# The last block of a fused attention and mixture kernel: where GpSimd multiplies, the order of two exponentials, and a product in two column halves

## The chip, the cores and the metric

The kernel runs on one core of one Trainium2 chip. The time is device microseconds (us) of one execution; of the kernel before three runs are known, 574.03, 574.24 and 574.85 us, median 574.24 us.

## What is computed

Three layers follow each other. Chunked attention takes chunks of 32 queries, each with a window of 56 keys and 8 memory keys. Its output x (3072 tokens, 512 wide) goes through a layer whose activation is a quotient of polynomials. Its result goes through a soft mixture of 8 experts with 4 slots each. Cut to what matters:

```python
h = x @ w_in                                   # 3072 x 2048
P = a0 + a1*h + a2*h**2 + a3*h**3
Q = 1 + |b0|*|h| + |b1|*h**2
g = P / (Q + 1e-6)
y = g @ w_out                                  # 3072 x 512

logits = y @ phi                               # 3072 x 32 slots
d = softmax of logits over the 3072 tokens     # one softmax per slot
slot_input = d.T @ y                           # 32 x 512
slot_out[e] = relu(slot_input[e] @ w1[e]) @ w2[e]   # 512 -> 1024 -> 512, per expert
c = softmax of logits over the 32 slots        # one softmax per token
out = c @ slot_out
```

## The kernel before, in words

The 3072 tokens are six blocks of 512, and the 2048 columns of h are eight steps of 256 in each block: 48 steps, 0 to 47. y is never formed. The logits come from g and w_out @ phi (the tile `wp`); d.T @ g is gathered in `u_acc`, and w_out is applied to that sum at the end.

A step's work is `run_step`. TensorE forms h (line 380). ScalarE takes |b0 h|, |b1| h squared and a3 h + a2 (lines 610, 611, 613), and turns Q into 1/Q by a logarithm and an exponential (627, 628). VectorE forms Q (612), the cubic's inner part (622, 623), and later (a0 + ...) / Q (635). GpSimd multiplies Q by 1/Q (588), and line 636 multiplies by 2 minus that product, which corrects the rounding of 1/Q. TensorE transposes g into the tiles `g` (405, copied at 406) and adds to the logits (398).

Once a block is through, `soft1` works on its logits: the largest value (424), the running minimum of the negated maxima (428), the factor `alpha` by which the old sums are rescaled (429), the exponential p with its sum (431), and beside these the softmax over slots (438 to 441). `soft2` transposes p (448, 450). `soft3` forms p times g (458) into a PSUM bank and adds it to `u_acc` (463; in the last block 467, in two column halves). In blocks 1 to 4 this lies among the steps of the block after; in the last one nothing follows to cover it.

The last two steps, 46 and 47, are `last_steps`. There the order of VectorE, ScalarE and GpSimd is the written one (`manual_schedule`); elsewhere a planner orders each engine's instructions by its own model of time, within the waits that the data ask for, and `issue_after(x)` makes instructions of the same engine queue behind x. `keep_busy` issues products whose result nobody reads (671).

Weights for the end come through SP's queue (line 575). `fill` and `fill_view` reuse tiles that are done with: in the order of the code the tiles `q`, `a4`, `k`, `v`, `xt`, `win` and `x`, and at the end `xt`, `T`, `S`, `T`, then the eight halves of the `g` tiles in `soft3` (470), `v`, and `win`. Each takes one piece of 512 KB: w_out's 8, w1's 32 and w2's 32. SP issues them in order, each when its tile is free. The half n = 0 of a `g` tile is its first two token groups (tt = 0, 1).

After `u_acc` come its transposes (758), the product with w_out (773), the experts (802, 839, 846) and the result, written by 12 transfers (878).

Of the kernel before, what the change touches and what calls it, by code (L numbers as in the profile page):

```python
# [12 lines left out]
AF = mybir.ActivationFunctionType  # L13
ALU = mybir.AluOpType
AX = mybir.AxisListType
# [31 lines left out]
def tile_chunk_attention__rational__soft_moe(  # L47
# [16 lines left out]
    PE, ACT, DVE, POOL, SP = nc.tensor, nc.scalar, nc.vector, nc.gpsimd, nc.sync  # L64

    NPAIR, P, HP, _ = qw.shape
# [9 lines left out]
    BLK = 512  # L76
    NBLK = NT // BLK
    TT = BLK // P
# [33 lines left out]
    def bank(shape):  # L112
        return ps_m("m", shape)
# [4 lines left out]
    ident = const("ident", [P, P])  # L118
# [3 lines left out]
    u_acc = const("u", [P, BLK])  # L122
# [137 lines left out]
    start = ExitStack()  # L260
# [123 lines left out]
    gts = {}  # L384
# [25 lines left out]
    den, alpha = run[:, 1:2], run[:, 3:4]  # L410

    def soft1(b):
        lgs = p_s2("s2", [P, BLK])
        ACT.activation(lgs, st["lg"], AF.Copy)
        lt = bank([P, BLK])
        PE.matmul(lt, lhsT=stack, rhs=lgs, start=True, stop=True)
        ct = bank([P, TT, NSLOT])
        for tt in range(TT):
            done = PE.matmul(ct[:, tt, :], lhsT=lgs[:, tt * P:tt * P + P], rhs=stack[:, 0:NSLOT], start=True, stop=True)
        if b == NBLK - 1:  # L420
            keep_busy(done.ins, 5)
        old, neg_m = (run[:, n:n + 1] for n in ((2, 0) if b % 2 else (0, 2)))
        bm, db = p_sm("bm", [P, 1]), p_sm("db", [P, 1])
        DVE.tensor_reduce(bm, lt, AX.X, ALU.max)
        if b == 0:
            DVE.tensor_scalar(neg_m, bm, -1.0, None, ALU.mult)
        else:
            DVE.tensor_scalar(neg_m, bm, -1.0, old, ALU.mult, ALU.min)
            ACT.activation(alpha, old, AF.Exp, bias=neg_m, scale=-1.0)
        pl = p_s2("s2", [P, BLK])  # L430
        ACT.activation(pl, lt, AF.Exp, bias=neg_m, accum_out=db)
        if b == 0:
            DVE.tensor_copy(den, db)
        else:
            DVE.tensor_scalar(den, den, alpha, db, ALU.mult, ALU.add)
        cm = p_sm("cm", [P, TT])
        ce = c_all[:, b, :].rearrange("p (t s) -> p t s", t=TT)
        DVE.tensor_reduce(cm, ct, AX.X, ALU.max)
        DVE.tensor_tensor(ce, ct, cm.unsqueeze(2).to_broadcast([P, TT, NSLOT]), ALU.subtract)
        ACT.activation(ce, ce, AF.Exp)  # L440
        DVE.tensor_reduce(csum[:, b * TT:b * TT + TT], ce, AX.X, ALU.add)
        st["pl"], st["ce"] = pl, ce
# [9 lines left out]
    def soft3(b):  # L452
        ce = st.pop("ce")
        p_tok = st.pop("ptok")
        pb = bank([P, BLK])
        for tt in range(TT):
            for j in range(4):
                PE.matmul(pb[32 * j:32 * j + 32, :], lhsT=p_tok[:, tt, :], rhs=gts[b, j][:, tt, :],  # L458
                          start=(tt == 0), stop=(tt == TT - 1))
        if b == 0:  # L460
            DVE.tensor_copy(u_acc, pb)
        elif b < NBLK - 1:
            DVE.scalar_tensor_tensor(u_acc, u_acc, alpha, pb, ALU.mult, ALU.add)
        else:
            for n in range(2):
                o = slice(BLK // 2 * n, BLK // 2 * n + BLK // 2)
                DVE.scalar_tensor_tensor(u_acc[:, o], u_acc[:, o], alpha, pb[:, o], ALU.mult, ALU.add)
            for n in range(2):
                for j in range(4):
                    fill_view(gts[b, j].rearrange("p t f -> p (t f)")[:, 1024 * n:1024 * n + 1024])  # L470
        for j in range(4):
            del gts[b, j]
        pb = bank([P, P])
        done = PE.transpose(pb, ce.rearrange("p t s -> p (t s)"), ident)
        if b == NBLK - 1:
            keep_busy(done.ins, 2)
        ACT.activation(c_all[:, b, :], pb, AF.Copy)
# [188 lines left out]
    def keep_busy(ins, n, rhs=None):  # L666
        if "t" not in idle:
            idle["t"] = ps_h("h", [P, 2, BLK])
        with tc.issue_after(ins):
            for _ in range(n):  # L670
                PE.matmul(idle["t"][:, 0, 0:P], lhsT=ident, rhs=ident if rhs is None else rhs, start=True, stop=True)

    def last_steps():
        k, z = total - 2, total - 1
        for what in "a1 h0 d1 p0 p1 t a2 h1".split():
            run_step(k, what)
        hh = hs.pop(z)
        s, t, y = p_S("S", [P, 2, BLK]), p_T("T", [P, 2, BLK]), p_S("S", [P, 2, BLK])
        w = p_S("S", [P, 2, BLK])
        t_, q_, w_ = late.pop(k)  # L680
        sums = ps_h("h", [P, BLK])
        POOL.memset(ctab[:, 5:6], QC * 2.0 ** -LN_SHIFT)
        for n in range(2):
            ACT.activation(s[:, n], hh[n], AF.Abs, scale=b0)
            ACT.activation(y[:, n], hh[n], AF.Square, scale=rb1)
            ACT.activation(t[:, n], hh[n], AF.Identity, bias=a2, scale=a3)
            if n:
                PE.matmul(sums, lhsT=ident, rhs=s[:, n], start=True, stop=False)
                PE.matmul(sums, lhsT=ident, rhs=y[:, n], start=False, stop=True)
            else:  # L690
                DVE.scalar_tensor_tensor(s[:, n], y[:, n], QC, s[:, n], ALU.add, ALU.add)
            POOL.tensor_tensor(y[:, n], q_[:, n], w_[:, n], ALU.mult)
            DVE.tensor_tensor(t[:, n], t[:, n], hh[n], ALU.mult)
            DVE.scalar_tensor_tensor(t[:, n], t[:, n], a1, hh[n], ALU.add, ALU.mult)
        for n in range(2):
            o = slice(n, n + 1)
            if n:
                ACT.activation(w[:, n], sums, AF.Ln, bias=ctab[:, 5:6], scale=2.0 ** -LN_SHIFT)
            else:
                ACT.activation(w[:, n], s[:, n], AF.Ln, scale=2.0 ** -LN_SHIFT)  # L700
            ACT.activation(w[:, o], w[:, o], AF.Exp, bias=ex_b, scale=-1.0)
            if n == 0:
                for part in range(2):
                    post(k - 1, part)
                keep_busy(st["turn"].ins, 12)
                keep_busy(st["turn"].ins, 7, w[:, 0, 0:P])
        DVE.scalar_tensor_tensor(t_, t_, a0, w_, ALU.add, ALU.mult)
        DVE.scalar_tensor_tensor(t_, y, 2.0, t_, ALU.subtract, ALU.mult, reverse0=True)
        for n in range(2):
            o = slice(n, n + 1)  # L710
            if n:
                DVE.scalar_tensor_tensor(s[:, n], sums, QC, w[:, n], ALU.add, ALU.mult)
            else:
                DVE.tensor_tensor(s[:, n], s[:, n], w[:, n], ALU.mult)
            DVE.scalar_tensor_tensor(t[:, o], t[:, o], a0, w[:, o], ALU.add, ALU.mult)
            DVE.scalar_tensor_tensor(t[:, o], s[:, o], 2.0, t[:, o], ALU.subtract, ALU.mult, reverse0=True)
        gt_tile[k], gt_tile[z] = t_, t

    for kk in range(total + 4):
        b, i = divmod(kk, NSTEP)  # L720
# [32 lines left out]
    end.enter_context(tc.manual_schedule(engines={PE.engine}))  # L753
    ut = p_s2("s2", [P, 4, P])
    turned = [bank([P, 2, P]) for _ in range(2)]
    for h in range(2):
        for n in range(2):
            done = PE.transpose(turned[h][:, n, :], u_acc[:, (2 * h + n) * P:(2 * h + n) * P + P], ident)
        if h:
            DVE.tensor_copy(ut[:, 2 * h:2 * h + 2, :], turned[h])  # L760
        else:
            ACT.activation(ut[:, 0:2, :], turned[h], AF.Copy)
    keep_busy(done.ins, 1)
    W = DM // 2
    sz = [wp.rearrange("p f s -> p (f s)")]
    POOL.memset(sz[0], 0.0)
# [1 line left out]
    pbs = [bank([P, W]) for _ in range(2)]  # L768

    def slots(w, ns):  # L770
        for n in ns:
            for j in range(4):
                PE.matmul(pbs[w][32 * j:32 * j + 32, :], lhsT=ut[:, n, 32 * j:32 * j + 32],
                          rhs=w_out_rows(4 * j + n)[:, W * w:W * w + W], start=(n == 0), stop=(n == 3))
# [7 lines left out]
        DVE.tensor_copy(by[:, :, :, 0:4], pb[:, :, 0:28].rearrange("p c (e s) -> p c e s", s=4))  # L782
        DVE.tensor_copy(z[:, :, 252:256], pb[:, :, 28:32])

    slots(0, range(4))
    ACT.activation(si[:, 0:W], pbs[0], AF.Copy, scale=rden)
    slots(1, range(2))
    slots_turned(0)
# [45 lines left out]
    for eq in range(2):  # L834
        for n in range(8 - 2 * eq):
            if eq == 0 and n in (2, 3):
                turn(1, n - 2)
            for j in range(4):
                PE.matmul(so[32 * j:32 * j + 32, :], lhsT=hts[eq][:, n, 32 * j:32 * j + 32],
                          rhs=got[("2", 4 * eq + j, n // 2)][:, n % 2, :],  # L840
                          start=(eq == 0 and n == 0), stop=False)
    for j in range(4):
        for n in range(2):
            for w in range(2):
                g = (j + 2 * n + w) % 4
                PE.matmul(so[32 * g:32 * g + 32, W * w:W * w + W], lhsT=hts[1][:, 6 + n, 32 * j:32 * j + 32],
                          rhs=got[("2", 4 + j, 3)][:, n, W * w:W * w + W],
                          start=False, stop=(j == 3))
# [4 lines left out]
    pb = [bank([P, W]) for _ in range(2)]  # L853
# [5 lines left out]
    for b in range(NBLK):  # L859
        for half in range(2):  # L860
            ob = p_win("win", [P, 2, DM])
            if half:
                pb = [bank([P, DM]) for _ in range(2)]
            else:
                both = ps_h("h", [P, 2, DM])
                pb = [both[:, m, :] for m in range(2)]
# [74 lines left out]
```

## Time and profile before

| what | value |
|---|---|
| median of three runs | 574.24 us (574.03 to 574.85) |
| the profiled execution | 573.23 us |
| its span, first to last instruction | 571.1 us |
| busy: TensorE, VectorE, ScalarE, GpSimd | 94%, 80%, 75%, 21% |
| mean granted TensorE clock | 0.984 of full speed |
| DMA moved | 105.80 MB, 185 GB/s over the span |

A start is in us from the span's start. In rows of instructions, "out<-in" are the program's tiles, L12 is line 12, and the bracket tells how long the engine sat idle before it and what ended that. A DMA row on SPq is the issue, and "to landing" is the time from the issue to the last part's arrival. The share of DMA is the mean busy share of 16 DMA engines (a little over 1 where packets overlap).

### The profile page before, as it was taken

Reading aid. Unit: us, or ns where it says so; the run is one execution under the profiler, and the core shown is the slowest. Engines: PE = TensorE matmul, PEld = TensorE weight load, DVE = VectorE, ACT = ScalarE, POOL = GpSimd, SP = SyncE. Lnnn points to the kernel's source line nnn. Section 1 sums busy time; section 2 is a strip of 40 time slices with the busy share of each in tenths; the row PEclk is TensorE's granted clock in tenths of the full one; section 3 lists DMA queues with packets and bytes.
Section 4 is the critical chain, followed back from the end, with each engine's and each line's share of the span. In section 5 each row is a group of like instructions: output and inputs, shape, how many; then the busy total and the mean of one; then the engine's idle time right before and its main releaser. Section 6 shows DMA issues by size and latency. Waiting matters only on the chain.

```text
span 571.1 us, 13640 instructions
## 1 busy us (share of the span) xinstructions
PE 537.9 (94%) x5874; PEld 360.2 (63%) x5874; DVE 455.7 (80%) x572; ACT 427.8 (75%) x551; POOL 122.8 (21%) x66
## 2 busy tenths in 40 slices
PE   6799899999999999999999999999999999999981
PEld 5654445467667677677766777776778667643351
DVE  4749999999989899979799799897898978831041
ACT  1669999998978899688887887878888978721132
POOL 0001111422213132313222213132323332300000
PEclk9699999999999999999999999999999999999997
DMA  8897763313225223533233315313359264799948
GB/s 322 352 393 268 259 223 117 116 64 113 63 86 185 76 80 143 185 112 94 93 112 111 133 57 183 112 48 138 111 178 376 94 239 147 293 397 409 408 163 355
DMA packets 28139, 105.80 MB, mean 185 GB/s; under 512 B 3376, under 2 KB 3504, under 8 KB 27056
## 3 DMA queue, kind: packets, MB, share of 16 engines
q1 hardware_dynamic: 26928, 100.74, 48.4%
q0 software_dynamic: 1152, 4.19, 1.8%
q8 instruction: 46, 0.75, 0.5%
q14 instruction: 13, 0.11, 0.1%
HBM read 94.44 MB, written 10.49 MB: 184 GB/s over the span
## 4 chain that ended last, share of the span: by engine, by line
PE 47%; DVE 25%; ACT 12%; DMA 7%; issue 6%; POOL 1%; SPq 1%; ACTq 0%; DVEq 0%; POOLq 0%
PE h L380 24%; PE m L405 4%; DMA win<-in_moe_w_dram 3%; DVE T L623 3%; PE lg L398 3%; DVE T L622 3%; PE m L458 3%; DVE S L612 3%; ACT S L610 3%; DVE T L635 3%; ACT S L611 2%; DVE T L636 2%; PE m L228 2%; DVE g L304 2%; DMA T<-in_moe_w_dram 2%
## 5 line engine op out<-in xcount | busy, mean ns | idle before, releaser
L380 PE MATMUL h<-xt,win 128*128 128x512 f32 x1012 | 266.8, 412 | 1.5 <-DVE T L623 1.3
L380 PEld LDWEIGHTS h<-xt,win 128*128 128x128 f32 x1012 | 183.7, 188 | 51.0 <-issue 12.3
L588 POOL TENSOR_TENSOR S<-S,S 128x1024 f32<-128x1024 f32 x46 | 112.8, 2452 | 329.5 <-DVE S L612 329.5
L610 ACT ACTIVATE S<-h,ctab 128x1024 f32<-128x1024 f32 x47 | 52.5, 1117 | 40.3 <-PE h L380 39.5
L612 DVE SCALAR_TENSOR_TENSOR S<-S,S 128x1024 f32<-128x1024 f32 x47 | 57.3, 1218 | 28.4 <-ACT S L611 28.2
L405 PEld LDWEIGHTS m<-ident,T 128*128 128x128 f32 x384 | 43.0, 141 | 30.7 <-issue 16.2
L622 DVE TENSOR_TENSOR T<-T,h 128x1024 f32<-128x1024 f32 x47 | 56.9, 1210 | 6.2 <-ACT T L613 6.2
L623 DVE SCALAR_TENSOR_TENSOR T<-T,ctab,h 128x1024 f32<-128x1024 f32 x47 | 59.8, 1271 | 0.7
L635 DVE SCALAR_TENSOR_TENSOR T<-T,ctab,S 128x1024 f32<-128x1024 f32 x46 | 58.6, 1274 | 0.0
L406 ACT ACTIVATE g<-m 128x512 f32<-128x512 f32 x96 | 53.5, 602 | 6.5 <-PE m L405 6.3
L636 DVE SCALAR_TENSOR_TENSOR T<-S,T 128x1024 f32<-128x1024 f32 x46 | 56.1, 1220 | 2.0
L613 ACT ACTIVATE T<-h,ctab 128x1024 f32<-128x1024 f32 x47 | 57.4, 1221 | 0.0
L405 PE MATMUL m<-ident,T 128*128 128x128 f32 x384 | 53.2, 277 | 3.0 <-DVE a L189 1.4
L628 ACT ACTIVATE S<-S,ctab 128x1024 f32<-128x1024 f32 x47 | 54.4, 1158 | 0.9
L627 ACT ACTIVATE S<-S 128x1024 f32<-128x1024 f32 x47 | 50.4, 1072 | 6.1 <-DVE S L612 6.1
L611 ACT ACTIVATE S<-h,ctab 128x1024 f32<-128x1024 f32 x47 | 52.7, 1121 | 1.4 <-DVE T L635 1.4
L398 PE MATMUL lg<-T,wp 128*32 128x512 f32 x192 | 37.3, 605 | 1.3 <-DVE T L636 0.7
L380 PE MATMUL h<-xt,x 128*128 128x512 f32 x64 | 30.7, 607 | 0.0
L190 ACT ACTIVATE a<-a 128x512 f32<-128x512 f32 x22 | 13.7, 631 | 14.6 <-DVE a L189 14.6
L458 PE MATMUL m<-g,s 128*32 128x512 f32 x192 | 22.0, 595 | 0.4 <-ACT s L450 0.4
L305 ACT ACTIVATE g<-g 128x1024 f32<-128x1024 f32 x16 | 18.8, 1173 | 2.1 <-DVE g L304 2.1
L228 PE MATMUL m<-v,a 64*32 64x64 f32 x1280 | 17.6, 224 | 1.3 <-issue 0.8
(218 smaller groups left out, 661.1 us busy)
## 6 DMA issues: line engine op xcount, KB each, us to landing
win<-in_moe_w_dram SPq DMA_DIRECT2D x31, 512.0 KB, 7.7
k<-in_kw_dram SPq DMA_DIRECT2D x22, 512.0 KB, 6.3
v<-in_vw_dram SPq DMA_DIRECT2D x22, 512.0 KB, 5.3
g<-in_moe_w_in_dram SPq DMA_DIRECT2D x16, 512.0 KB, 8.1
g<-in_w_turned_dram SPq DMA_DIRECT2D x16, 512.0 KB, 5.7
x<-in_moe_w_out_dram SPq DMA_DIRECT2D x8, 1024.0 KB, 4.9
out_dram<-win SPq DMA_DIRECT2D x12, 512.0 KB, 5.0
q<-in_qw_dram SPq DMA_DIRECT2D x11, 512.0 KB, 3.7
```

Source lines behind the costliest of these rows:

```text
L380: PE.matmul(tile_[f2] if step == total - 1 else tile_[:, f2, :], lhsT=ww[:, c, f2 * P:f2 * P + P], rhs=xx[:, c, :], start=(n == 0), stop=( ...
L398: PE.matmul(st["lg"][32 * j:32 * j + 32, :], lhsT=wp[:, 4 * qd + j, :], rhs=gt_tile[k - 1 + j // 2][:, j % 2, :], start=(qd == 0), stop=(q ...
L405: st["turn"] = PE.transpose(pb[:, m, f2 * P:f2 * P + P], t_[:, f2, tt * P:tt * P + P], ident)
L588: POOL.tensor_tensor(out, q, w, ALU.mult)
L610: ACT.activation(s, hh, AF.Abs, scale=b0)
L611: ACT.activation(y, hh, AF.Square, scale=rb1)
L612: pins[0] = DVE.scalar_tensor_tensor(s, y, QC, s, ALU.add, ALU.add).ins
L613: pins[1] = ACT.activation(t, hh, AF.Identity, bias=a2, scale=a3).ins
L622: DVE.tensor_tensor(t, t, hh, ALU.mult)
L623: behind[kk] = DVE.scalar_tensor_tensor(t, t, a1, hh, ALU.add, ALU.mult).ins
L635: DVE.scalar_tensor_tensor(t, t, a0, w, ALU.add, ALU.mult)
L636: st["t"] = DVE.scalar_tensor_tensor(t, e, 2.0, t, ALU.subtract, ALU.mult, reverse0=True).ins
```

## The change

There are four edits.

- In `soft1` of blocks 1 to 5 the exponential p is issued before `alpha`, and `alpha` queues behind it. In the last block the maximum over slots (438) queues behind the running minimum (428).
- In `soft3` of the last block the product of p and g is two products of 256 columns, each into a PSUM bank of its own. Each half of `u_acc` is added from its own bank.
- In `last_steps` GpSimd's product for step 46 is one instruction of 1024 columns, ahead of the work of step 47, in place in `q_`. It was two of 512 columns into the two halves of step 47's tile `y`, each after that half had been used.
- At the end the transposes of `u_acc` are issued by a function, called just ahead of the product with w_out, and one `keep_busy` of one product is gone. The product's first four parts stand as two and two, in the same order.

```diff
         else:
-            DVE.tensor_scalar(neg_m, bm, -1.0, old, ALU.mult, ALU.min)
-            ACT.activation(alpha, old, AF.Exp, bias=neg_m, scale=-1.0)
+            behind_m = DVE.tensor_scalar(neg_m, bm, -1.0, old, ALU.mult, ALU.min).ins
         pl = p_s2("s2", [P, BLK])
-        ACT.activation(pl, lt, AF.Exp, bias=neg_m, accum_out=db)
+        behind_p = ACT.activation(pl, lt, AF.Exp, bias=neg_m, accum_out=db).ins
+        if b:
+            with tc.issue_after(behind_p):
+                ACT.activation(alpha, old, AF.Exp, bias=neg_m, scale=-1.0)
...
-        DVE.tensor_reduce(cm, ct, AX.X, ALU.max)
+        with tc.issue_after(behind_m) if b == NBLK - 1 else nullcontext():
+            DVE.tensor_reduce(cm, ct, AX.X, ALU.max)
...
-        pb = bank([P, BLK])
-        for tt in range(TT):
-            for j in range(4):
-                PE.matmul(pb[32 * j:32 * j + 32, :], lhsT=p_tok[:, tt, :], rhs=gts[b, j][:, tt, :],
-                          start=(tt == 0), stop=(tt == TT - 1))
+        parts = 2 if b == NBLK - 1 else 1
+        pbs = []
+        for n in range(parts):
+            o = slice(BLK // parts * n, BLK // parts * (n + 1))
+            pbs.append(bank([P, BLK // parts]))
+            for tt in range(TT):
+                for j in range(4):
+                    PE.matmul(pbs[n][32 * j:32 * j + 32, :], lhsT=p_tok[:, tt, :], rhs=gts[b, j][:, tt, o],
+                              start=(tt == 0), stop=(tt == TT - 1))
+        pb = pbs[0]
...
-                DVE.scalar_tensor_tensor(u_acc[:, o], u_acc[:, o], alpha, pb[:, o], ALU.mult, ALU.add)
+                DVE.scalar_tensor_tensor(u_acc[:, o], u_acc[:, o], alpha, pbs[n], ALU.mult, ALU.add)
...
         POOL.memset(ctab[:, 5:6], QC * 2.0 ** -LN_SHIFT)
+        POOL.tensor_tensor(q_, q_, w_, ALU.mult)
         for n in range(2):
...
-            POOL.tensor_tensor(y[:, n], q_[:, n], w_[:, n], ALU.mult)
...
-        DVE.scalar_tensor_tensor(t_, y, 2.0, t_, ALU.subtract, ALU.mult, reverse0=True)
+        DVE.scalar_tensor_tensor(t_, q_, 2.0, t_, ALU.subtract, ALU.mult, reverse0=True)
...
-    for h in range(2):
+
+    def u_turned(h):
         for n in range(2):
-            done = PE.transpose(turned[h][:, n, :], u_acc[:, (2 * h + n) * P:(2 * h + n) * P + P], ident)
+            PE.transpose(turned[h][:, n, :], u_acc[:, (2 * h + n) * P:(2 * h + n) * P + P], ident)
...
-    keep_busy(done.ins, 1)
+
...
-    slots(0, range(4))
+    u_turned(0)
+    u_turned(1)
+    slots(0, range(2))
+    slots(0, range(2, 4))
```

## Rows read from the trace of the kernel before

**Rows 1.** The chain of waits, 512 to 548 us: start, us, what.
```profile
512.21 2.73 PE m L773 x48
...
517.44 9.63 DMA win<-in_moe_w_dram
...
537.37 10.04 DMA T<-in_moe_w_dram
...
547.46 0.68 PE lg L846 x8
```
**Rows 2.** Busy time by stretch; the last three columns are TensorE's clock, DMA share, GB/s.
```profile
508.00:512.00 4.00, 3.96 (x35) 1.76 (x27) 0.87 (x2) 0.65 (x2) 0.00 (x0) 1.00 0.96 354
509.50:510.00 0.50, 0.50 (x12) 0.00 (x0) 0.00 (x0) 0.00 (x0) 0.00 (x0) 1.00 0.70 246
512.00:544.00 32.00, 32.00 (x318) 11.56 (x321) 3.77 (x9) 3.35 (x7) 0.53 (x1) 1.00 1.03 410
544.00:548.00 4.00, 3.68 (x52) 1.27 (x44) 0.00 (x0) 0.00 (x0) 0.00 (x0) 1.00 0.31 126
```
**Rows 3.** Line 575 at 487.0, at 502.9 and at 508.7 us: issues, then landing.
```profile
L575 SPq DMA_DIRECT2D win<-in_moe_w_dram x1: 328/328/328, 487.0 to 487.0; - x1
...
DMA to landing us min/median/max: 3.6/3.6/3.6
...
L575 SPq DMA_DIRECT2D T<-in_moe_w_dram x1: 327/327/327, 502.9 to 502.9; - x1
...
DMA to landing us min/median/max: 10.1/10.1/10.1
...
L575 SPq DMA_DIRECT2D g<-in_moe_w_dram x1: 328/328/328, 508.7 to 508.7; - x1
...
DMA to landing us min/median/max: 5.6/5.6/5.6
```
**Rows 4.** Waits of SP's own queue, 503 to 520 us: total, times, longest.
```profile
SPq L575 <- PE m L458: 4.7, 1, 4.7
```
**Rows 5.** Instructions in order of time, steps 46 and 47.
```profile
486.83 1.15 ACT L628 ACTIVATE S<-S,ctab 128x1024 f32<-128x1024 f32 x1
486.93 1.28 DVE L635 SCALAR_TENSOR_TENSOR T<-T,ctab,S 128x1024 f32<-128x1024 f32 x1
...
488.32 1.23 DVE L636 SCALAR_TENSOR_TENSOR T<-S,T 128x1024 f32<-128x1024 f32 x1
...
493.04 1.28 DVE L707 SCALAR_TENSOR_TENSOR T<-T,ctab,S 128x1024 f32<-128x1024 f32 x1
...
495.49 1.23 DVE L708 SCALAR_TENSOR_TENSOR T<-S,T 128x1024 f32<-128x1024 f32 x1 [1.16 <-POOL S L692]
...
495.91 1.73 PE L671 MATMUL h<-S,ident 128*128 128x128 f32 x14
...
500.74 1.05 PE L398 MATMUL lg<-T,wp 128*32 128x512 f32 x2 [0.57 <-DVE T L716]
```
**Rows 6.** Lines 692 and 304 over the span: ns min/median/max, first and last start.
```profile
L692 POOL TENSOR_TENSOR S<-S,S x2: 1276/1624/1971, 490.3 to 493.5; 128x512 f32<-128x512 f32 x2
...
L304 DVE TENSOR_SCALAR g<-g x16: 662/694/2560, 20.0 to 123.5; 128x1024 f32<-128x1024 f32 x16
```
**Rows 7.** Instructions in order of time, the last block's softmax and product.
```profile
504.45 0.29 DVE L438 TENSOR_REDUCE cm<-m 128x4 f32<-128x128 f32 x1
504.65 0.20 DVE L428 TENSOR_SCALAR run<-bm,run 128x1 f32<-128x1 f32 x1
...
504.89 0.29 ACT L429 ACTIVATE run<-run 128x1 f32<-128x1 f32 x1 [1.50 <-DVE run L428]
505.10 0.67 ACT L431 ACTIVATE s<-m,run 128x512 f32<-128x512 f32 x1
...
506.77 3.64 PE L458 MATMUL m<-g,s 128*32 128x512 f32 x32 [0.43 <-ACT s L450]
```
**Rows 8.** VectorE in order of time, block 4: the sum that needs alpha.
```profile
452.89 0.27 DVE L435 TENSOR_SCALAR run<-run,db 128x1 f32<-128x1 f32 x1
```

## The prediction

> **What bounds the kernel now.** The busy shares (TensorE 94%) point at TensorE, but they average over stages. The change is almost all in the last 85 us, so I read the chain of waits there first. The reader is to see that from 517.44 us on it holds no engine but three transfers in a row, each about 10 us, and that the first product behind them starts at 547.46 [rows 1]. Then the stretches: from 512 to 544 us the DMA share is 1.03 and 410 GB/s flow without a dip, with the clock granted in full [rows 2]. So the stage is held by the weights of the experts. A piece is 524,288 bytes, at 410 GB/s 1.28 us; that no engine shows faster work here counts for nothing as long as the pieces follow each other.
>
> The question is whether the pieces could follow each other better. There is one dip: from 508 to 512 us the rate is 354 GB/s, which lacks (410 - 354) x 4 us = 224 KB or 0.55 us [rows 2]. It stands where SP waited 4.7 us, its longest wait there, for the product of p and g to free the first `g` tile [rows 4]. At first sight those 0.55 us are what the change can win.
>
> The landings say something else [rows 3]. The last piece before that wait was issued at 502.9 and landed 10.1 us later, at 513.0. The first `g` piece was issued at 508.7 and landed 5.6 us later, at 514.3. That is 1.3 us behind the former, one piece's time. Yet at 509.5 to 510.0 only 0.70 of the engines were busy [rows 2]. Both hold if the engines are not level: some had run dry at 509.5, while the slowest one, whose part decides when a piece has landed, still worked on older pieces until 513 and never stood still. The end of the stream says the same: from 544 to 548 the share is 0.31 and only 0.5 MB come in (126 GB/s x 4 us) [rows 2], while the last piece is awaited until 547.41 (537.37 + 10.04) [rows 1]. So the dip costs the fast engines time, and the end belongs to a slow one that has no dip.
>
> How late may the first `g` piece be? On an idle queue a piece landed 3.6 us after its issue (487.0) [rows 3]. It now lands at 514.3, so an issue up to 514.3 - 3.6 = 510.7 us changes nothing. This is the point from which the chain ahead decides; the first issue is at 508.7, 2.0 us sooner.
>
> **The change part by part.** All times are of the profiled execution, 573.23 us: a span of 571.1 and 2.13 around it. The median of the runs is 1.01 above it, and I add that at the end.
>
> *GpSimd's product.* VectorE's line 708 waited 1.16 us for it [rows 5]. In place, the product needs only the exponential of step 46, which ends at 486.83 + 1.15 = 487.98, so it can run from there for about 2.4 us (two halves alone, 2 x 1.28 = 2.55 [rows 6]) and is long done when line 707 ends at 494.32. The 1.16 us go from VectorE's chain. What is late next is TensorE: its idle products last until 495.91 + 1.73 = 497.64, so the transposes of step 46 can't come sooner, and of the last logits' product at 500.74 only its own wait of 0.57 us [rows 5] is sure to go. Bounds: 0.57 to 1.16 us sooner, or, with the port below, later. I take 0.6, the row of the wait itself.
>
> Against this stands an overlap. The second half of the old product took 1971 ns, the first 1276 [rows 6]; the second ran beside line 707, which reads two SBUF tiles from 493.04 to 494.32 [rows 5]. Line 304 took 2560 ns at worst against a median of 694 [rows 6]. The new product would be asked for at 487.98, while line 635 runs until 488.21, and line 636, again with two SBUF tiles, comes at 488.32 [rows 5]. If GpSimd goes in between, line 636 waits until 488.21 + 2.4 = 490.6 in place of 488.32: 2.3 us, and the logits' product of step 45 and all behind it, the idle products too, with it. The Trainium skill, page "SBUF — State Buffer", section "Who interferes with whom", states that a VectorE instruction with two SBUF inputs and a GpSimd one that reads SBUF exclude each other for a whole instruction; the 1971 ns agree, and by that rule the chain would lose the 2.3 us. No row shows GpSimd waiting between two such VectorE instructions, so which of the two goes first is open. Bounds of this edit: 1.16 us sooner to 2.3 us later.
>
> *Softmax.* With line 438 behind line 428, its 0.29 us leave the way to p; with `alpha` behind p, 505.10 - 504.89 = 0.21 us more [rows 7]. Sum 0.5 us sooner. Line 438 and `alpha` now run beside the transposes and the product; `alpha` is next needed by line 467, over 3 us later, and would cost its 0.29 us if that cover were gone. In blocks 1 to 4 the swap costs nothing if ScalarE fits `alpha` in before VectorE's line 435, which shows no idle time ahead of it in block 4 [rows 8]; if not, up to 0.29 us each.
>
> *Two column halves.* The product takes 3.64 us for 4 token groups of 512 columns [rows 7]. 48 instructions of 256 columns took 2.73 us [rows 1]; 64 of them take 3.64. So the whole is as long as before, but the first four `g` halves, free until now after two of four groups (506.77 + 1.82 = 508.59, issued at 508.7), are read again by the second half's groups 0 and 1: 3.64 x 6/8 = 2.73 us after the start, 0.91 us later. The later four come at the product's end as before. The gain is that the first half of `u_acc` is ready 1.8 us sooner; TensorE is in the second half then, so only the second half's sum stands before the transposes, some 0.4 us. The second PSUM bank was the softmax's, read long before.
>
> *The removed idle product* and the calls' order: 0.2 to 0.4 us sooner at the product with w_out. The clock was granted in full from 508 us on [rows 2], and TensorE is as busy as before with twice as many half-length products, so I count nothing for it.
>
> *The sum.* First `g` issue: 508.7 - 0.6 - 0.5 + 0.9 = 508.5 us; with the port 508.7 + 2.3 - 0.5 + 0.9 = 511.4. The first is 2.2 us ahead of 510.7, the second 0.7 us behind it. The slots' product starts over 1 us sooner, but from 517.44 on transfers alone stand in the chain. The S tiles' fills come some us sooner, into a queue that already holds several pieces. So nothing is left of the gain: 573.23 + 0 in the profile, 574.24 + 0 = 574.2 us.
>
> **The rivals.**
>
> *The slow engine doesn't fall behind (0.15).* Why it was behind no row tells. If the moved fills change that, all engines end level. After 544 us there are 0.5 MB, 1.23 us at 410 GB/s, so the last byte would come at 545.2, against a landing at 547.41: up to 2.2 us, less some tail of the landing. I take 1.6: 572.6 us. For it: the dip shows engines that are ahead. Against it: the order of the pieces is the same, and the slow ones fell behind before any tile that the change frees sooner could have been filled.
>
> *The port (0.10 beyond what can be told).* At line 636 GpSimd's product goes first. The price is nothing up to a first `g` issue at 510.7 and then one us for one us: with the softmax's gain 511.4 and 0.7 us (574.9), without it 508.7 + 2.3 + 0.9 = 511.9 and 1.2 us (575.4). For it: GpSimd waits while line 635 still runs. Against it: line 636 follows within 0.11 us, and part of the price is given back as line 708 no longer waits.
>
> *The swap in the middle blocks (0.05).* `alpha` comes too late for line 435 in each of blocks 1 to 4, and VectorE holds up the steps there: 4 x 0.29 = 1.2 us, 575.4 us. It decides only if TensorE then waits. Against it: line 435 did not wait.
>
> *The change doesn't shorten the chain*, as the planner leaves TensorE's idle products ahead: 508.7 - 0.5 + 0.9 = 509.1, still ahead of 510.7, 574.2 us, and so part of the forecast.
>
> **How the numbers follow.** About 0.2%, 1.15 us, is what a measurement of this kernel can tell from no change. The forecast has 0.70, with its own range of 573.4 to 575.0 (the runs before spread over 0.8 us, and the port's 0.7 lies in it). The first rival's 0.15 is faster; I add 0.01 for a chain that counts after all. The port's 0.10 and the swap's 0.05 are slower, less the 0.01. The range reaches to 572.3, below the first rival, and to 575.6, above the other two.
>
> **What would show it.** Right: line 708 without its wait, line 431 directly behind 428, the first `g` issue between 507.9 and 509.1 us, the dip about as deep, and yet the last piece landing within 0.5 us of 547.4. The port: line 636 lasting over 2 us, or the product well over 2.4. Wrong: the last landing sooner by as much as the `g` issue, which would make the issue and not the slow engine the bound; or a step of blocks 1 to 4 that got longer.

## The result, and the profile after

The changed kernel took 578.08 us (median of 6 runs, 577.04 to 579.29) against 574.13 (573.28 to 574.85) of the one before on the same chip: a ratio of 1.0074 [1.0060, 1.0088], 4 us slower. On one of the three chips of the experiments, where the runs spread more widely (572.8 to 577.7 for the kernel before), it was 577.02 against 573.99, 1.0047 [1.0027, 1.0068]. The profiled execution took 577.7 us with a span of 575.6, 4.5 us more than the span before. Lines from 431 on stand some lines lower: `soft3`'s product is line 465 (458 before), its sum 475 (467), the fills 583 (575), the last factor of a step 644 (636), step 47's 716 (708), step 47's sums in PSUM 697 and 698 (688 and 689), the idle products 679 (671).

The chain of waits of the changed kernel (start, us, what) answers to [rows 1].
```profile
489.45 3.19 DVE T L644
492.69 1.05 PE lg L398 x4
...
510.23 3.66 PE m L465 x64
...
514.28 6.91 DMA g<-in_moe_w_dram
...
541.77 10.11 DMA T<-in_moe_w_dram
551.92 0.68 PE lg L858 x8
```
The reader is to see two things. A VectorE instruction of 3.2 us stands where instructions of 1.23 stood. And transfers still end the chain, but the last piece lands at 551.88 (541.77 + 10.11), 4.47 us later than before [rows 1]. From the first `lg` product behind that on, nothing changed: the first output leaves 5.6 us behind the last landing in both traces.

Executions differ in when the last steps begin at all. A mark that none of the four edits touches is the first `win` fill of [rows 3], at 487.02 before and at 488.13 after; in the traces of the kernels below it stands between 486.4 and 489.5. I count from it. Of the 4.47 us, 1.11 were there already. The other 3.36 are the change's: the last landing is 63.75 us behind the mark instead of 60.39, and the first `g` issue 24.91 (513.04) instead of 21.68.

The changed kernel's instructions in order of time answer to [rows 5] and [rows 7].
```profile
489.17 2.38 POOL L691 TENSOR_TENSOR S<-S,S 128x1024 f32<-128x1024 f32 x1 [0.88 <-ACT S L636]
489.45 3.18 DVE L644 SCALAR_TENSOR_TENSOR T<-S,T 128x1024 f32<-128x1024 f32 x1
492.69 1.05 PE L398 MATMUL lg<-T,wp 128*32 128x512 f32 x4 [2.69 <-DVE T L644]
493.67 1.54 PE L405 MATMUL m<-ident,T 128*128 128x128 f32 x8
495.00 1.92 PE L697 MATMUL h<-S,ident 128*128 128x512 f32 x2
496.71 1.46 PE L698 MATMUL h<-S,ident 128*128 128x512 f32 x2
497.30 1.23 DVE L716 SCALAR_TENSOR_TENSOR T<-S,T 128x1024 f32<-128x1024 f32 x1
...
508.19 0.21 DVE L428 TENSOR_SCALAR run<-bm,run 128x1 f32<-128x1 f32 x1
...
508.52 0.69 ACT L430 ACTIVATE s<-m,run 128x512 f32<-128x512 f32 x1 [1.30 <-DVE run L428]
510.23 3.66 PE L465 MATMUL m<-g,s 128*32 128x256 f32 x64 [0.43 <-ACT s L453]
```
GpSimd's product begins at 489.17, line 644 at 489.45. The product ends at 491.55 and line 644 at 492.63, 1.1 us behind it, as if it had done its work only then. Its 45 other executions take about 1226 ns. Step 47's factor (716) has lost its wait of 1.16 us, as it was meant to; p (430) comes straight behind the minimum (428).

Busy time by stretch of the changed kernel; the last three columns are TensorE's granted clock, the DMA share and GB/s. They answer to [rows 2].
```profile
491.00:493.00 2.00, 0.32 (x2) 0.14 (x4) 2.00 (x2) 1.74 (x3) 0.55 (x1) 1.00 0.95 326
493.00:495.00 2.00, 2.00 (x12) 1.33 (x9) 1.97 (x4) 1.70 (x3) 0.00 (x0) 0.79 0.92 358
495.00:497.00 2.00, 2.00 (x4) 0.97 (x4) 1.96 (x3) 0.73 (x2) 0.00 (x0) 0.50 1.02 399
497.00:499.00 2.00, 2.00 (x11) 1.25 (x11) 1.89 (x3) 0.70 (x2) 0.00 (x0) 0.86 1.02 412
...
511.00:513.00 2.00, 2.00 (x44) 1.20 (x40) 0.48 (x1) 0.00 (x0) 0.00 (x0) 1.00 0.11 39
513.00:515.00 2.00, 2.00 (x29) 1.22 (x17) 0.48 (x1) 0.37 (x2) 0.00 (x0) 1.00 0.38 74
...
517.00:519.00 2.00, 2.00 (x36) 1.21 (x30) 0.19 (x2) 0.47 (x1) 0.00 (x0) 1.00 1.03 322
```
Behind TensorE's idle 2.69 us the clock fell to 0.50, its lower level of 1.2 GHz; before, it was 1.00 from 488 to 502 us. From 511 to 515 us the DMA engines moved only 39 and then 74 GB/s, and 4 us behind the restart there is a second dip, 322 GB/s. The share there is 1.03, so the engines are busy in it and move less. SP waited 6.3 us for the product in place of the 4.7 of [rows 4]:
```profile
SPq L583 <- PE m L465: 6.3, 1, 6.3
```
The first `g` piece, at 513.0 us, answers to the last of [rows 3]: it landed after 3.5 us, as on an idle queue (3.6 at 487.0). The third, at 514.28, took 6.91 and stands in the chain above.
```profile
L583 SPq DMA_DIRECT2D g<-in_moe_w_dram x1: 327/327/327, 513.0 to 513.0; - x1
...
DMA to landing us min/median/max: 3.5/3.5/3.5
```

**The 3.23 us of the first `g` issue**, stage by stage between starts in the two traces:

| stage | before | after | difference |
|---|---|---|---|
| mark to step 45's last logits (398) | 2.58 | 4.56 | +1.98: line 644 |
| to the idle products (671 / 679) | 3.64 | 5.31 | +1.67: the clock |
| to the slots' maxima (416) | 9.23 | 8.30 | -0.93: no wait of line 398 for `T` |
| to the product p times g | 4.30 | 3.93 | -0.37: softmax |
| to the first `g` issue | 1.93 | 2.81 | +0.88: halves |

### The profile page after: what moved, and what is told of

The parts are those of the page before. It is cut to its first block, busy times and chain, and to the rows that moved or that the text cites. A ratio compares the mean times of both kernels' runs of the same rounds, so it can differ in the third digit from the quotient of the medians.

```text
span 575.6 us, 13702 instructions
## 1 busy us (share of the span) xinstructions
PE 539.7 (94%) x5904; PEld 362.0 (63%) x5904; DVE 457.8 (80%) x572; ACT 428.3 (74%) x551; POOL 122.0 (21%) x65
## 4 chain that ended last, share of the span: by engine, by line
PE 52%; DVE 20%; ACT 12%; DMA 8%; issue 5%; POOL 1%; SPq 0%; ACTq 0%; DVEq 0%; POOLq 0%
PE h L380 28%; PE m L405 4%; DMA win<-in_moe_w_dram 4%; PE lg L398 3%; PE m L465 3%; DVE T L631 3%; ACT S L618 3%; DVE T L630 3%; DVE S L620 2%; ACT S L619 2%; DVE T L643 2%; ACT g L406 2%; DVE T L644 2%; PE m L228 2%; DMA T<-in_moe_w_dram 2%
## 5 line engine op out<-in xcount | busy, mean ns | idle before, releaser
L631 DVE SCALAR_TENSOR_TENSOR T<-T,ctab,h 128x1024 f32<-128x1024 f32 x47 | 59.8, 1272 | 0.7
L644 DVE SCALAR_TENSOR_TENSOR T<-S,T 128x1024 f32<-128x1024 f32 x46 | 58.1, 1263 | 2.0
L465 PE MATMUL m<-g,s 128*32 128x512 f32 (+1 forms) x224 | 22.0, 534 | 0.4 <-ACT s L453 0.4
```

What stands on the lines that cost most here:

```text
L631: behind[kk] = DVE.scalar_tensor_tensor(t, t, a1, hh, ALU.add, ALU.mult).ins
L644: st["t"] = DVE.scalar_tensor_tensor(t, e, 2.0, t, ALU.subtract, ALU.mult, reverse0=True).ins
```

## The experiments

My theory after the result: GpSimd's product goes in ahead of line 644, TensorE idles and its clock falls, the halves add their 0.9 us, and the late `g` issue runs the DMA queue dry, which the end pays for. The rivals: the stream's end has another cause; the clock alone is to blame; the swap in the middle blocks costs time. "Mark" is the first `win` fill.

| kernel | first `g` issue | last landing | us, against before on the same chip | ratio |
|---|---|---|---|---|
| before | 21.7 | 60.4 | | |
| product alone | 22.7 | 60.8 | 575.94 / 573.96 | 1.0037 [1.0019, 1.0056] |
| halves alone | 22.6 | 61.4 | 575.31 / 573.96 | 1.0020 [1.0003, 1.0037] |
| softmax alone | 21.3 | 59.7 | 573.33 / 573.79 | 0.9996 [0.9976, 1.0016] |
| change without the product | 22.2 | 60.4 | 575.07 / 573.96 | 1.0014 [0.9994, 1.0035] |
| change, product held back | 21.3 | 60.2 | 573.86 / 573.96 | 0.9991 [0.9977, 1.0005] |
| the same without halves | 20.4 | 60.0 | 573.37 / 573.99 | 0.9983 [0.9966, 1.0000] |
| before, late `g` fills | 24.8 | 63.2 | 576.24 / 573.99 | 1.0034 [1.0013, 1.0055] |
| change, TensorE kept busy | 23.0 | 62.2 | 574.98 / 573.96 | 1.0016 [0.9999, 1.0033] |
| change once more | 24.7 | 63.9 | 577.02 / 573.99 | 1.0047 [1.0027, 1.0068] |

(First issue and last landing in us behind the mark, from one profiled execution each; the times are medians of 10 or 12 runs, against 17 to 31 of the kernel before.)

**The product alone.**
```diff
         POOL.memset(ctab[:, 5:6], QC * 2.0 ** -LN_SHIFT)
+        POOL.tensor_tensor(q_, q_, w_, ALU.mult)
...
-            POOL.tensor_tensor(y[:, n], q_[:, n], w_[:, n], ALU.mult)
...
-        DVE.scalar_tensor_tensor(t_, y, 2.0, t_, ALU.subtract, ALU.mult, reverse0=True)
+        DVE.scalar_tensor_tensor(t_, q_, 2.0, t_, ALU.subtract, ALU.mult, reverse0=True)
```


> The kernel before with one edit: GpSimd's product in place and ahead of step 47's work. Theory (the port): line 636 waits behind GpSimd's product and lasts about 3.2 us in place of 1.23, TensorE idles some 2.7 us for it and works at the lower clock for a few us after; the first g issue comes 2 to 3 us later than before (before: 508.7), near 511.5, past the 510.7 at which the slowest DMA engine runs dry. Then 575 to 577.5 us. Rival 1 (the column halves are the cause): alone the product costs nothing, 574.1 within 0.5 us. Rival 2 (the swapped exponentials in blocks 1 to 4): nothing here either, 574.1 us.

The last factor of a step in this kernel (its line 636): ns min/median/max, first and last start.
```profile
L636 DVE SCALAR_TENSOR_TENSOR T<-S,T x46: 1175/1226/3180, 60.8 to 489.4; 128x1024 f32<-128x1024 f32 x46
```
The 3180 ns stand in the one execution that meets the product. So the product makes them, with no other edit near. TensorE again idled 2.7 us, yet here the granted clock stayed at 1.00 in the two stretches behind it:
```profile
491.00:493.00 2.00, 0.33 (x2) 0.14 (x4) 2.00 (x2) 1.74 (x3) 0.53 (x1) 1.00 0.83 262
493.00:495.00 2.00, 2.00 (x13) 1.13 (x10) 1.97 (x4) 1.72 (x3) 0.00 (x0) 1.00 0.87 268
```
The first `g` issue is 1.0 us later: 1.98 less 0.93, without the clock's part. From step 45's last logits to the idle products this trace takes 3.63 us, as before the change (3.64), against 5.31 in the changed kernel with the same order of work, so that the clock makes those 1.67 us:
```profile
492.67 1.05 PE L398 MATMUL lg<-T,wp 128*32 128x512 f32 x4 [2.68 <-DVE T L636]
...
496.30 2.84 PE L671 MATMUL h<-ident 128*128 128x128 f32 x24
```
The profiled execution, 574.84 us, was one of the faster ones of this kernel; whether the clock fell in the others no trace tells.

**The two halves alone**, with the end as in the change.
```diff
-        pb = bank([P, BLK])
+        parts = 2 if b == NBLK - 1 else 1
...
-    keep_busy(done.ins, 1)
...
+    u_turned(0)
+    u_turned(1)
```


> The kernel before with one edit: the last block's product with g in two column halves, with the transposes' new place. Theory (the port): the first g issue comes 0.9 us later, 509.6, still ahead of 510.7, so the slowest DMA engine doesn't run dry: 574.1 within 0.6 us. Rival 1 (halves): the later g issue alone lets the queue run dry, 575.5 us or more.

The first issue came 0.9 us later and still 1.1 us ahead of my limit (510.7, which is 23.7 behind the mark). The end was 1.0 us later all the same and the time 0.20% longer. The stretches of this kernel:
```profile
510.00:512.00 2.00, 2.00 (x32) 1.30 (x21) 0.48 (x1) 0.28 (x1) 0.00 (x0) 1.00 0.60 166
512.00:514.00 2.00, 1.73 (x31) 0.97 (x33) 0.43 (x1) 0.38 (x1) 0.00 (x0) 1.00 0.98 371
514.00:516.00 2.00, 2.00 (x36) 1.20 (x31) 0.00 (x0) 0.47 (x1) 0.00 (x0) 1.00 0.95 250
```
The dip is deeper than before's, and 4 us behind the restart there is a second one, 250 GB/s at a share of 0.95, while the queue holds pieces. By the limit nothing of this should have reached the end. The interval ends close to 1; the late fills and the busy TensorE below bear the finding out with larger effects.

**The softmax's order alone** (the edit in `soft1`).
```diff
-            ACT.activation(alpha, old, AF.Exp, bias=neg_m, scale=-1.0)
...
+        if b:
+            with tc.issue_after(behind_p):
+                ACT.activation(alpha, old, AF.Exp, bias=neg_m, scale=-1.0)
```


> The kernel before with one edit: the order of the two exponentials in blocks 1 to 5, and of lines 428 and 438 in the last. Theory (only the first g issue matters): the first g issue comes 0.4 to 0.5 us sooner after the first fill of step 47's tiles (21.2 in place of 21.7), 573.7 to 574.0 us, no difference that can be told. Rival (the swap holds up the steps of blocks 1 to 4): the steps there are longer by up to 0.3 us each and the time is 574.5 to 575.3 us.

The first issue 0.4 us sooner, the time the same within its interval. The swap costs the middle blocks nothing that can be measured.

**The change without the product's edit** (softmax, halves and the end).
```diff
-        POOL.tensor_tensor(q_, q_, w_, ALU.mult)
...
+            POOL.tensor_tensor(y[:, n], q_[:, n], w_[:, n], ALU.mult)
```


> The changed kernel with GpSimd's product as it was before (two halves into y). Theory (the port): line 636's time is back at 1.23 us, first g issue near 508.7 - 0.4 + 0.9 = 509.2, 574.1 within 0.6 us. Rival 1 (halves): still 2 to 4 us slower than before. Rival 2 (swap in blocks 1 to 4): about 1.1 us slower than before, with the same lag in the steps ahead of 487 us.

1.0014, which can't be told from no change. Beside the change's 1.0047 on this chip that leaves most of the loss to the product.

**The change with the product held back.** A one-column product that reads VectorE's sum of step 47's first half makes GpSimd start only when VectorE has passed line 644.
```diff
-        POOL.tensor_tensor(q_, q_, w_, ALU.mult)
...
                 DVE.scalar_tensor_tensor(s[:, n], y[:, n], QC, s[:, n], ALU.add, ALU.add)
+                hold = p_sm("hold", [P, 1])
+                POOL.tensor_tensor(hold, s[:, 0, 0:1], s[:, 0, 0:1], ALU.mult)
+                POOL.tensor_tensor(q_, q_, w_, ALU.mult)
```


> The changed kernel, but GpSimd's product (whole, in place) is held by a one-column GpSimd product that reads what VectorE's sum of step 47's first half has written, so it runs beside VectorE instructions that read PSUM. Theory (the port): line 636's work takes 1.23 us, the product ends near 492.7 us, line 708's work doesn't wait, TensorE's clock stays at its upper level, the first g issue comes near 508.5, and the time is 574.0 within 0.6 us: the chain is shorter than before but the transfers set the end. Rival 1 (halves): 576 us or more. Rival 3 (the chain counts in full): 572.5 us, as 1.6 us leave the chain.

Line 644 of this kernel, and its product in order of time:
```profile
L644 DVE SCALAR_TENSOR_TENSOR T<-S,T x46: 1160/1226/1227, 60.3 to 488.5; 128x1024 f32<-128x1024 f32 x46
```
```profile
490.58 2.36 POOL L702 TENSOR_TENSOR S<-S,S 128x1024 f32<-128x1024 f32 x1
```
The product starts 3.36 us behind the mark (487.22 in this trace) instead of 1.04, 2.3 us later, and the whole loss is gone: 0.9991. The same instruction with the same operands costs nothing there. This shows the product's place as the cause.

**The same without the halves.**
```diff
-        parts = 2 if b == NBLK - 1 else 1
...
+        pb = bank([P, BLK])
...
+    keep_busy(done.ins, 1)
```


> The changed kernel with GpSimd's product held (as in the run before of that name) and the last block's product with g in one piece, as before the change. Theory: the first g issue comes about 20.4 us after the first fill of step 47's tiles (before: 21.7), the dip of the DMA rate near 510 us is gone, and as the slowest DMA engine sets the end the time stays at 574.0 within 0.6 us. Rival (the issue sets the end): faster by 0.5 us or more.

First issue 20.4, 1.3 us sooner than before, and no dip is left:
```profile
510.00:512.00 2.00, 1.96 (x16) 0.89 (x9) 0.87 (x2) 0.30 (x2) 0.00 (x0) 1.00 1.02 406
```
It is worth 0.4 us at the last landing and 0.9983 [0.9966, 1.0000] in time. That is the best that the edits gave, and hardly to be told from no change.

**Late `g` fills alone.** On the kernel before, a 2 KB transfer out of `u_acc` stands in SP's queue ahead of the `g` fills and holds them until the sum is through. No engine's work is changed.
```diff
+    late_dr = p_dr("late", [1, BLK])
...
+            SP.dma_start(out=late_dr, in_=u_acc[0:1, :])
             for n in range(2):
```


> The kernel before with one transfer of 2 KB (a row of the finished sum u_acc to DRAM) put into SP's queue ahead of the g fills, so that these wait for line 467's end and come about 3 us later (near 511.8 us, or 24.8 after the first fill of step 47's tiles, as in the changed kernel), while no engine's work changes. Theory (the late issue alone makes the time): slower by 1.2 us for the dry queue and up to 2 us more as the slowest engine loses time again some 4 us after the restart: 575.2 to 577.5. Rival (the longer chain of engines itself counts, the transfers don't): 574.1 within 0.5 us.

The hold in this kernel's waits of SP:
```profile
SPq L469 <- DVE u L468: 8.4, 1, 8.4
```
With the first issue at 24.8, as late as in the change, the last landing is 63.2 behind the mark against the change's 63.8, with the softmax, TensorE and its clock as before. So a late queue, with no engine later than before, is enough for 2.8 of the 3.4 us.

How much passes to the end can be read in one stretch for four kernels, 20 to 34 us behind the mark, and in the last 3 us ahead of the last landing. Before, then the change, halves alone, late fills:
```profile
507.02:521.02 14.00, 13.96 (x155) 6.28 (x151) 1.88 (x7) 1.61 (x4) 0.53 (x1) 1.00 1.01 397
544.41:547.41 3.00, 2.72 (x40) 1.00 (x32) 0.00 (x0) 0.00 (x0) 0.00 (x0) 1.00 0.28 111
```
```profile
508.13:522.13 14.00, 13.30 (x180) 7.97 (x183) 3.48 (x16) 3.05 (x9) 0.53 (x1) 1.00 0.77 284
548.88:551.88 3.00, 1.82 (x28) 0.43 (x20) 0.00 (x0) 0.00 (x0) 0.00 (x0) 1.00 0.33 131
```
```profile
507.70:521.70 14.00, 13.73 (x185) 7.01 (x181) 1.96 (x7) 1.61 (x4) 0.53 (x1) 1.00 0.95 349
546.07:549.07 3.00, 1.82 (x28) 0.45 (x20) 0.00 (x0) 0.00 (x0) 0.00 (x0) 1.00 0.43 171
```
```profile
507.09:521.09 14.00, 13.96 (x155) 6.29 (x151) 1.88 (x7) 1.61 (x4) 0.53 (x1) 1.00 0.79 305
547.32:550.32 3.00, 1.60 (x18) 0.32 (x16) 0.00 (x0) 0.00 (x0) 0.00 (x0) 1.00 0.42 169
```
And the change without the product's edit, the first of the two stretches:
```profile
509.02:523.02 14.00, 13.73 (x185) 6.90 (x177) 1.97 (x7) 1.61 (x4) 0.53 (x1) 1.00 0.97 381
```
The change moved (397 - 284) x 14 us = 1.58 MB less, 3.9 us at 410 GB/s; its landing is 3.36 later. The halves lack 0.67 MB or 1.6 us, for 1.0; the late fills 1.29 MB or 3.1 us, for 2.8. Part of what the end takes in is a fuller last stretch: 131, 171 and 169 GB/s instead of 111, 0.15 to 0.44 us. The change without the product lacks 0.22 MB or 0.55 us and lands when the kernel before does (60.42 and 60.39); softmax alone lacks nothing and lands 0.7 us sooner. So single traces scatter by some 0.6 us: a dip of 1.6 us or more passes to the end for the most part, and what becomes of one of half a us these traces can't tell.

**The change with TensorE kept busy.** Twelve idle products stand behind step 47's last h product; with them the written order put step 47's sums ahead of step 45's logits.
```diff
+        with tc.issue_after(st["hp"]):
+            for _ in range(12):
+                PE.matmul(sums[:, 0:P], lhsT=ident, rhs=ident, start=True, stop=True)
```


> The changed kernel with 12 idle products more on TensorE, behind step 47's product, so that TensorE does not stand idle while line 644 is kept waiting (they go ahead of the sums of step 47, which with them come before the logits' product of step 45). Theory (part of the loss is the lower clock behind the 2.7 us of idleness): the granted clock stays at 1.00 from 488 to 500 us, line 644 still lasts about 3.2 us, the first g issue comes about 1.7 us sooner than in the changed kernel (near 23.2 after the first fill in place of 24.8), and the time is 575 to 576 us. Rival (the clock costs nothing beside the wait): first g issue near 24.8 and 577 to 578 us as before.

The stretches of this kernel:
```profile
490.00:492.00 2.00, 2.00 (x8) 0.58 (x11) 2.00 (x3) 1.47 (x3) 0.00 (x0) 1.00 0.98 309
492.00:494.00 2.00, 2.00 (x20) 1.33 (x13) 1.93 (x4) 1.47 (x4) 0.00 (x0) 1.00 0.99 369
```
The clock held, line 644 still lasted 3187 ns, and the first issue came 2.0 us sooner than in the change: the 1.67 us of the clock, as the table of stages has them, and some of the other order. The two causes are thus separate, the clock being the second link. The first issue is 0.7 us ahead of my limit, and yet the last landing is 1.8 us later than before.

**The change once more**, without an edit.

> The changed kernel once more, for a second trace. Theory (the port): line 636's work (line 644 there) again lasts about 3.2 us and TensorE idles 2.7 us for it; the granted clock may or may not fall behind that, as it did in the first trace and did not with the product alone. With the fall the first g issue is about 24.9 us after the first fill, without it about 23.2, and the last landing 63.7 or about 61.5. Rival (the first trace's order of things was chance): line 644 takes 1.23 us.

Line 644 again had one execution of 3177 ns, and the clock fell again:
```profile
492.00:494.00 2.00, 1.42 (x4) 0.19 (x4) 1.97 (x4) 1.44 (x3) 0.00 (x0) 0.60 0.97 291
494.00:496.00 2.00, 2.00 (x10) 1.57 (x9) 1.97 (x4) 0.96 (x2) 0.00 (x0) 0.54 0.94 356
```

**Why does an engine fall behind at all?** In the kernel before there is a drop 4 us behind the mark too, at a full queue:
```profile
491.00:493.00 2.00, 2.00 (x11) 1.28 (x10) 1.84 (x3) 1.97 (x4) 0.57 (x1) 1.00 0.80 264
```
One idea was that engines that have stood idle start unevenly. So transfers were put ahead of the mark: five of 256 KB, then three of 512 KB, on the kernel before, then the three on the version with the product held back and no halves.
```diff
+    awake_dr = p_dr("awake", [3, P, 2, 4 * P])
...
+        if k == total - 4 and part == 0:
+            for m in range(3):
+                SP.dma_start(out=awake_dr[m], in_=gts[b, qd - 1][:, 0:2, :])
```


> The kernel before with five transfers of 256 KB from a g tile to unused DRAM put into SP's queue ahead of the two fills that wait for step 47's product, so that the DMA engines are not idle from 484 to 488 us. Theory (an idle queue makes one or a few engines fall 2 to 4 us behind some 4 us after it restarts): without the idle stretch that lag is gone or smaller, the last piece lands 1 to 3 us sooner after the first fill than the 60.4 us of before, 571.5 to 573.5 us. Rival (the lag has another cause, as the engines' own load): the last landing stays at 60 to 61 us after the first fill, 574.1 within 0.6 us, or later by what the extra transfers hold up.

> The kernel before with three transfers of 512 KB from a g tile that is long complete to unused DRAM, issued right behind the last fill ahead of step 47 (near 480 us), so that the DMA engines work until about 487 us and the fills of step 47's tiles are not held up. Theory (an engine falls behind because the queue restarts from idle): the drop of the rate some 4 us after the first fill is gone, the last landing comes 57.5 to 59.5 us after the first fill in place of 60.4, and the time is 571.5 to 573.3 us. Rival (the lag comes with any burst of fills): last landing at 60 to 61 and 574.0 within 0.6 us.

> The version that the experiments point to: the changed kernel with GpSimd's product held behind VectorE's sum, the product with g in one piece, and the three early transfers that keep the DMA engines at work. Theory: the first g issue near 20.4 after the first fill, no dip near 510 us, the last landing 57 to 59 us after the first fill, 570.5 to 573 us. Rival (only the earlier issue helps, not the kept-awake queue): 573.4 us, as with the product held and no halves.

The five came late, at 485.74, and put off the mark to 489.46; 574.22 against 573.99 us, 1.0003 [0.9986, 1.0021]. The three: 573.32 against 573.96, 0.9982 [0.9966, 0.9998]; with the held product 572.79 against 573.96, 0.9986 [0.9967, 1.0005]. The stretches of the kernel with the three:
```profile
487.00:489.00 2.00, 2.00 (x11) 1.14 (x10) 1.94 (x2) 1.97 (x3) 0.89 (x2) 1.00 0.38 137
492.00:494.00 2.00, 2.00 (x9) 1.04 (x8) 1.85 (x4) 1.97 (x5) 0.30 (x1) 1.00 0.96 305
```
Behind the early transfers there is a gap, 487 to 489, and 4 us behind the mark the drop is there as before, 305 GB/s; with the held product 270, from 491 to 494 us. So the drop doesn't need a long idle time ahead. It doesn't come with each burst of fills either: with the product held and no halves the eight `g` fills met a queue still at work, and from 512 to 516 us, 3 to 7 us behind the first of them, the rate is 414 and 406 GB/s. In these traces it stands only behind a gap. The last landings of the three are 59.2 (behind a mark that was itself put off), 59.8 and 60.0 us behind the mark; the 57 to 59.5 of the theory came only for the five, behind their late mark, and not in the time. No version beats the kernel before by more than 0.18%, with intervals that end at its time or next to it.

## Why the prediction was wrong

It said 574.2 us, no change, with 572.3 to 575.6; 578.08 came.

**A step that failed: "an issue up to 514.3 - 3.6 = 510.7 us changes nothing".** I read that a slow DMA engine never stood still, so that the end had 2.0 us of room. The landing times are as I read them, but the conclusion isn't. The halves alone kept 1.1 us clear of that limit and cost 1.0 us at the end; the change with TensorE kept busy was 0.7 us clear of it, and 1.8 us late at the end; the late fills alone, 1.1 us beyond it, cost 2.8. Of what a dip of that size lacks in bytes most passes to the end. I had taken a lag of one piece at one moment for a room that lasts; behind each restart the rate drops anew, 4 us later. This step made the port look cheap, 0.7 to 1.2 us. By itself it would not have moved the forecast: without the limit, and one us for one us, the sum's 508.5 is 0.2 us sooner than 508.7, the halves' +0.9 (0.88 measured) included.

**The step that decided: the sum takes GpSimd's product as 0.6 us sooner and leaves the port to a rival of 0.10.** The port is what came. The mechanism was in the text with its place and was priced at 2.3 us for line 636; it measured 1.95 (3.18 - 1.23). With the product held and the rest as in the change, the sum came out: the first `g` issue at 21.3 behind the mark, where the forecast's 508.5 is 21.5, and a time of 0.9991. With the port's own 511.4 and one us for one us the forecast would have been 574.24 + 2.7 = 576.9. The Trainium skill, page "SBUF — State Buffer", section "Who interferes with whom", has a VectorE instruction with two SBUF inputs and GpSimd's reading of SBUF exclude each other for a whole instruction; the trace agrees, with 3.18 or 3.19 us in four traces and 1.23 where the product was held. What I argued against it, that line 636 follows within 0.11 us, spoke for a close race and not for its outcome: GpSimd's product began at 489.17, and line 643, the instruction ahead of 644, ended at 489.34 (488.06 + 1.28). GpSimd came first and stayed first. The price behind the limit was then wrong with the limit: 0.7 to 1.2 us where the last landing came 3.4 later.

**The clock was in no step.** I looked at it from 508 us on only and wrote that it was granted in full. TensorE's wait of 2.69 us at 490 us made the next products slower by 1.67 us in the execution profiled, half of what the `g` issue lost; in the trace of the product alone, where the clock stayed up, the same stage lost nothing. A stall put on TensorE has to be priced with the clock behind it.

**The smaller terms** held: the gain at line 398 was 0.93 (I took 0.6, bound 1.16); the softmax 0.37 (0.5): 0.29 from the maximum as said, but 0.12 for `alpha` in place of 0.21, and 0.04 given back. The swap in the middle blocks cost nothing: in block 4 of the changed kernel `alpha` ends at 453.41 and VectorE's sum, which answers to [rows 8], starts without idle time at 454.00:
```profile
453.07 0.34 ACT L433 ACTIVATE run<-run 128x1 f32<-128x1 f32 x1
454.00 0.27 DVE L437 TENSOR_SCALAR run<-run,db 128x1 f32<-128x1 f32 x1
```
The clock at TensorE's product with w_out held, as forecast. The softmax's gain alone could not be told in time, as its interval is 0.2% to either side.

**What the account of the end left out: TensorE is close behind the transfers.** I read in [rows 2] that the transfers flow without a dip from 512 to 544 us; TensorE is busy there for all of the 32.00 us too, and it waited only 0.32 us for the last piece. In the trace of the product alone the profile shows no wait for a piece: its last products came straight behind the ones before, 60.95 us behind the mark instead of 60.44, though the last piece had landed at 60.8. Before, then the product alone:
```profile
547.46 0.64 PE L846 MATMUL lg<-T,k 128*32 128x256 f32 x8 [0.32 <-DMA T<-in_moe_w_dram]
```
```profile
549.08 0.61 PE L846 MATMUL lg<-T,k 128*32 128x256 f32 x8
```
In the changed kernel the transfers end the chain. But its product with w_out starts 27.2 us behind the mark instead of 25.1, here before and after:
```profile
512.14 0.40 PE L773 MATMUL m<-q,s 128*32 128x256 f32 x1
```
```profile
515.35 0.40 PE L782 MATMUL m<-q,s 128*32 128x256 f32 x1 [0.28 <-ACT s L771]
```
In the product alone that start is 1.0 us later than before and the last products 0.5, so the end takes in some 0.5 us. By an estimate from these rows TensorE's own chain would have made the change 2.1 - 0.5 = 1.6 us later even with every piece on time.

**What stays open:** why the transfers' rate drops some 4 us behind a restart; and what decides whether the clock falls behind the same idle time, as it did in two of three traces.

## What to carry to other kernels

Where a stream of transfers sets the end, expect a dip to be paid for there for the most part, as those of 1.6 us and more were here; a late piece is no room to spend, and a tile that such a stream refills must not be read longer for the sake of an engine. Before moving a GpSimd instruction with SBUF operands earlier, look which VectorE instructions with two SBUF inputs it will stand beside, and take it that the one that asked first holds the other for its whole length; behind the last of them it cost nothing here. Look at the engine that uses the stream, too: where it is busy without a gap, it may be the next limit within half a us. Price a new wait of TensorE with the slower clock that may follow it.

## What was unexpected of the hardware

Line 644, in one place of 46, took 3.18 us beside a GpSimd product of 2.38 that had started 0.28 us before it, and 1.23 without it. Behind 2.7 us of idle TensorE the clock fell to its lower level in two of three traces of the same order of work; eight transposes then took 1.54 us instead of 1.09, four sums 3.38 instead of 2.04. And a queue that starts again after a gap drops about 4 us later, for some 2 us, to 250 to 322 GB/s in the stretches shown, though pieces are waiting and the DMA share is 0.80 to 1.03. The traces' records of single packets tell where the time goes. A packet of 4 KB mostly takes 0.16 us. In the first 7 us behind the mark, 9 to 22 of them in each trace take 0.5 to 1.7 us; from 7 to 20 us behind it none does in any trace. Behind the first `g` issue up to 25 do so again, up to 1.8 us, and none in the three kernels whose `g` fills met a queue still at work (first issue 19.6 and 20.4 us behind the mark).
